# Eight clamps of a weight-narrowing chain issued from GpSimd instead of VectorE

## The chip, the cores and the metric

The kernel runs on one core of a Trainium2 chip. The metric is the device time of one execution in microseconds (us); before the change it is 867.72 us, the median of three runs (867.5 to 868.18).

## The reference

The inputs are `q`, `k`, `v` of shape (4, 8, 576, 64), and two pairs of weights `w_in` (512 x 2048) and `w_out` (2048 x 512). What is computed is a retention attention followed by two dense layers:

```python
scores = scale * np.matmul(q, k.transpose(0, 1, 3, 2))
ret = scores * Dmat[None]            # gamma_h ** (i - j) below the diagonal
x = np.matmul(ret, v)                # to (2304, 512) tokens
h = x @ w1_in;  x = np.maximum(0.01 * h, h) @ w1_out
h = x @ w2_in;  out = (h - np.tanh(h)) @ w2_out
```

The weights arrive as 64-bit floats, seen on the chip as 64-bit words; everything else is 32-bit.

## The kernel before, in words

The work has two parts. `retention()` goes over 16 pairs of heads (four batches of four pairs), and from pair 5 on it interleaves layer 1's first weight group with them, in twelve "units". `layers()` then does the rest of the two layers, and is bound to the order that a list of steps gives. Every engine executes its instructions in the order in which the program issues them; the order is written out by hand (`tc.manual_schedule()`).

**Pairs.** In pair i the program issues: the loads of pair i + 2 on SyncE's queue; `scores(i)` (TensorE, line 632, into the single PSUM tile `sc`); `prep_q(i)` (GpSimd, lines 602 and 607, two products that scale q in place); `mask(i)` (VectorE, line 646, two products from `sc`, which must be done before `scores(i + 1)` may write `sc`); then fillers; then `pair_steps(i)`, which has a unit's first matmuls `unit_h(u)` (line 758, into the single PSUM tile `x_b`), fillers, the second matmuls of the unit before, `unit_o(u - 1)` (line 783), then the outputs of pair i - 1 (lines 697 and 708), the states of pair i (lines 665, 673, 675), the copies out of PSUM (lines 716, 717), the mask of the tail (line 655) and the preparation of pair i + 1 (lines 621, 613); then fillers again. Behind `unit_h(u)` ScalarE and VectorE read `x_b` (lines 764 to 766), so `unit_h(u + 1)` must wait for line 766 of unit u.

**Fillers.** `fill(i, part)` issues the next stretch of a list of operations that narrows weight pieces from 64 to 32 bits. The first 8 pieces of the list are layer 1's first weight group: pieces 0 and 1 are the first two input blocks, 2 and 3 the first two output blocks, 4 and 5 input, 6 and 7 output. `narrow_ops` gives five operations for each piece:

- `begin` (ScalarE, line 166): the absolute value of the top words goes to a tile `cw`. The pool of `cw` has two buffers here, so `begin` of piece n + 2 waits until the split of piece n has read its tile.
- `clamp` (VectorE, line 172): `cw` is bounded from below and above, in place.
- `shift` (VectorE, line 177): a shift and a bit mask, in place.
- `top` and `low` (VectorE, line 183, twice): the sign and the low bits are joined in from the landed 64-bit words.

`split_piece` follows later: ScalarE rounds `cw` into a matmul weight (line 255), GpSimd subtracts for the low part (line 256). Between a piece's `shift` and its `top` stands the split of the piece before. Which operation falls into which pair is set by the list `at_pair = [0, 4, 9, 15, 22, 34, 46, 52]`. For what follows, by that list: `clamp` 0 is issued in pair 1; `low` 0, `clamp` 1 and `shift` 1 in pair 2; split 0, `top` 1, `low` 1 and `clamp` 2 in pair 3; `shift` 2, split 1, `top` 2, `low` 2 and `clamp` 3 in pair 4; `shift` 3, split 2, `top` 3, `low` 3 and then, behind `unit_h(0)`, `clamp` 4 and the rest of piece 4 in pair 5; pieces 5 and 6 in pair 6, piece 7 in pair 7, and split 7 in pair 8.

**Who needs them.** `unit_h(0)` in pair 5 and `unit_h(1)` in pair 6 multiply by pieces 0 and 1, `unit_o(0)` in pair 6 by pieces 2 and 3, `unit_h(2)` in pair 7 by pieces 4 and 5, and `unit_o(2)` in pair 8 by pieces 6 and 7. Later pieces are narrowed by the same `narrow_ops`, 56 of them with a clamp, and keep VectorE for it.

Of the kernel before, what the change touches and what calls it, by code (L numbers as in the profile page):

```python
# [35 lines left out]
def retention_moe_moe(  # L36
# [16 lines left out]
    nc = tc.nc  # L53
# [9 lines left out]
    GF = 4  # L63
# [88 lines left out]
    def narrow_ops(key):  # L152

        if not wide:
            def only():
                w = cw_pool[0].tile([P, 512], F32, tag="cw", name="cw")
                nc.vector.tensor_copy(out=w, in_=raw.pop(key))
                half[key] = w
            return [only]
        t = {}  # L160

        def begin():
            words = raw.pop(key).bitcast(U32).rearrange("p (n t) -> p n t", t=2)
            t["lo"], t["hi"] = words[:, :, 0], words[:, :, 1]
            t["w"] = cw_pool[0].tile([P, 512], U32, tag="cw", name="cw")
            nc.scalar.activation(  # L166
                out=t["w"].bitcast(F32), in_=t["hi"].bitcast(F32), func=AF.Abs
            )

        def clamp():  # L170
            wf = t["w"].bitcast(F32)
            nc.vector.tensor_scalar(  # L172
                out=wf, in0=wf, scalar1=F64_LO, scalar2=F64_HI, op0=ALU.max, op1=ALU.min
            )

        def shift():
            nc.vector.tensor_scalar(
                out=t["w"], in0=t["w"], scalar1=3, scalar2=0x3FFFFFF8,
                op0=ALU.logical_shift_left, op1=ALU.bitwise_and,
            )  # L180

        def join(src, scalar, op):
            nc.vector.scalar_tensor_tensor(  # L183
                out=t["w"], in0=t[src], scalar=scalar, in1=t["w"], op0=op, op1=ALU.bitwise_or
            )

        def top():
            join("hi", 0xC0000000, ALU.bitwise_and)

        def low():  # L190
            join("lo", 29, ALU.logical_shift_right)
            half[key] = t["w"].bitcast(F32)

        return [begin, clamp, shift, top, low]

    def keep_split(key, wf):
# [916 lines left out]
```

## Time and profile before

| | |
|---|---|
| median of three runs | 867.72 us (867.5 to 868.18) |
| the profiled execution, whole | 868.1 us |
| its span, first to last instruction | 866.1 us |
| mean granted TensorE clock | 0.998 of full speed |
| busy: TensorE | 850.1 us (98%) |
| busy: VectorE | 604.1 us (70%) |
| busy: ScalarE | 451.2 us (52%) |
| busy: GpSimd | 377.1 us (44%) |

The profile is one execution. Its time of 868.1 us is 0.38 us above the median, and 2.0 us of it lie outside the span. Times within the span count from its first instruction. In a timeline row the columns are start, duration, engine, line, operation, output from inputs, shapes and the number of merged instructions; the bracket at the end says how long the engine sat idle ahead of the row, and what released it. Engine names there are PE (TensorE), PEld (its weight loads), DVE (VectorE), ACT (ScalarE), POOL (GpSimd) and SP (SyncE).

### The profile page before, as it was taken

The numbers are of one execution on the slowest core, as the hardware profiler recorded it, in microseconds if no ns is written. First come the engines' busy times: TensorE is split into PE (matmuls) and PEld (weight loads), VectorE is DVE, ScalarE is ACT, GpSimd is POOL, SyncE is SP. The second block draws the span as 40 slices with busy tenths as digits, with TensorE's granted clock in tenths as the row PEclk, the third lists the DMA queues.
The fourth block names the chain that finished last, engine by engine and source line by source line (L and its number), as shares of the span: only waits on it lengthen the run. The fifth ranks groups of instructions, "written<-read, shape, count | busy, mean of one in ns | idle before, by whom it ended". The sixth has DMA issues, their size and how long they took to land.

```text
span 866.1 us, 15237 instructions
## 1 busy us (share of the span) xinstructions
PE 850.1 (98%) x5728; PEld 748.2 (86%) x5728; DVE 604.1 (70%) x1038; ACT 451.2 (52%) x899; POOL 377.1 (44%) x304
## 2 busy tenths in 40 slices
PE   6999999999999999999999999999999999999997
PEld 5889999888888889888888898888999899999996
DVE  5995767587786676658765577756676667777675
ACT  4553444453255433454444577666556566566663
POOL 2541222040036302464365379655545445545553
PEclk9999999999999999999999999999999999999999
DMA  9835663433454533644444503572225412563112
GB/s 340 315 125 172 219 209 118 150 121 103 135 213 186 179 121 110 243 170 127 190 175 165 195 1 146 226 284 75 75 96 180 162 73 74 208 231 121 49 50 74
DMA packets 38778, 134.43 MB, mean 155 GB/s; under 512 B 4400, under 2 KB 5936, under 8 KB 36656
## 3 DMA queue, kind: packets, MB, share of 16 engines
q1 hardware_dynamic: 38272, 133.25, 43.7%
q8 instruction: 45, 0.74, 0.4%
q14 instruction: 29, 0.24, 0.1%
q10 hardware_dynamic: 432, 0.20, 0.1%
HBM read 97.26 MB, written 36.18 MB: 154 GB/s over the span
## 4 chain that ended last, share of the span: by engine, by line
PE 89%; DVE 4%; DMA 2%; issue 2%; POOL 1%; ACT 1%; POOLq 0%; ACTq 0%; SPq 0%; DVEq 0%
PE a L428 40%; PE h L275 22%; PE h L309 17%; PE a L783 3%; PE x_b L758 3%; PE o L708 1%; PE sc L632 1%; PE o L697 1%; DVE cw L183 1%; DMA acc<-in_w1i 1%; DMA cm_sb<-in_cmask 1%; DVE pt L646 1%; PE x_c L665 0%; DVE v L394 0%; DMA kt_sb<-in_ktab 0%
## 5 line engine op out<-in xcount | busy, mean ns | idle before, releaser
L428 PE MATMUL a<-w 128*128 128x512 f32 (+1 forms) x1680 | 395.2, 377 | 0.5 <-POOL w L400 0.5
L428 PEld LDWEIGHTS a<-w 128*128 128x128 f32 x1680 | 293.1, 188 | 48.9 <-POOL w L400 1.3
L256 POOL TENSOR_TENSOR w<-cw,w 128x512 fp32r<-128x512 f32 x80 | 113.5, 1436 | 233.6 <-ACT w L255 207.8
L275 PE MATMUL h<-xh,w 128*128 128x512 f32 (+1 forms) x672 | 187.1, 349 | 0.0
L368 POOL TENSOR_TENSOR v<-t,u 128x512 f32<-128x512 f32 (+1 forms) x76 | 93.1, 1225 | 100.5 <-ACT t L365 96.4
L275 PEld LDWEIGHTS h<-xh,w 128*128 128x128 f32 x672 | 119.5, 188 | 17.0
L400 POOL TENSOR_TENSOR w<-v,w 128x512 fp32r<-128x512 f32 (+1 forms) x76 | 96.1, 1265 | 63.9 <-ACT w L399 63.9
L354 ACT ACTIVATE w<-h 128x512 fp32r<-128x512 f32 (+1 forms) x68 | 37.2, 547 | 160.3 <-PE h L275 115.4
L275 PE MATMUL h<-xl,w 128*128 128x512 f32 (+1 forms) x336 | 117.0, 348 | 0.0
L309 PE MATMUL h<-xh,w 128*128 128x256 f32 x512 | 100.9, 281 | 0.2
L309 PEld LDWEIGHTS h<-xe,w 128*128 128x128 f32 x576 | 80.8, 189 | 10.7 <-DVE mk L303 3.1
L183 DVE SCALAR_TENSOR_TENSOR cw<-st,cw 128x512 uint32<-128x512 uint32 x96 | 86.4, 900 | 2.5
L394 DVE SCALAR_TENSOR_TENSOR v<-q,v 128x512 f32<-128x512 f32 (+1 forms) x76 | 60.8, 800 | 37.1 <-POOL v L368 37.1
L364 ACT ACTIVATE u<-h 128x512 f32<-128x512 f32 (+1 forms) x80 | 44.2, 553 | 80.4 <-DVE h L303 53.2
L309 PEld LDWEIGHTS h<-xh,w 128*128 128x128 f32 x512 | 83.1, 190 | 2.8 <-DVE v L397 1.5
L309 PE MATMUL h<-xe,w 128*128 128x256 f32 x576 | 84.3, 282 | 1.1 <-DVE mk L303 1.0
L505 DVE TENSOR_TENSOR acc<-a,acc 128x512 f32<-128x512 f32 (+1 forms) x114 | 72.1, 657 | 18.5 <-PE a L428 18.5
L399 ACT ACTIVATE w<-v 128x512 fp32r<-128x512 f32 (+1 forms) x76 | 45.3, 596 | 61.5 <-DVE v L397 59.0
L172 DVE TENSOR_SCALAR cw<-cw 128x512 f32<-128x512 f32 x64 | 33.1, 518 | 57.7 <-ACT cw L166 57.6
L309 PE MATMUL h<-xl,w 128*128 128x256 f32 x256 | 71.8, 281 | 0.0
L275 PEld LDWEIGHTS h<-xl,w 128*128 128x128 f32 x336 | 63.3, 188 | 8.6
L383 DVE TENSOR_TENSOR h<-h,t 128x512 f32<-128x512 f32 (+1 forms) x80 | 51.3, 641 | 15.2 <-ACT t L365 15.2
(82 smaller groups left out, 1159.8 us busy)
## 6 DMA issues: line engine op xcount, KB each, us to landing
kept<-w SPq DMA_DIRECT2D x48, 512.0 KB, 3.5
w<-kept SPq DMA_DIRECT2D x48, 512.0 KB, 4.8
xe<-xkept SPq DMA_DIRECT2D x12, 1536.0 KB, 6.7
st<-in_w2i SPq DMA_DIRECT2D x16, 512.0 KB, 3.5
st<-in_w1i SPq DMA_DIRECT2D x12, 512.0 KB, 4.1
st<-in_w1o SPq DMA_DIRECT2D x12, 512.0 KB, 3.5
xkept<-xe SPq DMA_DIRECT2D x4, 1536.0 KB, 6.7
kv<-in_vn SPq DMA_DIRECT2D x16, 320.0 KB, 5.2
```

Source lines behind the costliest of these rows:

```text
L183: nc.vector.scalar_tensor_tensor(out=t["w"], in0=t[src], scalar=scalar, in1=t["w"], op0=op, op1=ALU.bitwise_or)
L256: nc.gpsimd.tensor_tensor(out=wp[:, 1, :], in0=wf, in1=wp[:, 0, :].bitcast(F32), op=ALU.subtract)
L275: nc.tensor.matmul(out=ps[:, :n], lhsT=w[:, wi, cs], rhs=x[:, kk, t0:t0 + n], start=kk == 0 and i == 0, stop=kk == KK - 1 and i == 2,)
L309: nc.tensor.matmul(out=out_, lhsT=w[:, wi_, at:at + P], rhs=x(xi, kk), start=start and kk == 0 and j == 0, stop=stop and kk == 1 and j == ...
L364: nc.scalar.activation(out=u[:, :n], in_=h, func=AF.Square)
L368: nc.gpsimd.tensor_tensor(out=v[:, :n], in0=t_[:, :n], in1=u[:, :n], op=ALU.mult)
L383: nc.vector.tensor_tensor(out=h, in0=h, in1=tmp[s][1][:, :n], op=ALU.subtract)
L394: nc.vector.scalar_tensor_tensor(out=v, in0=q, scalar=RHO_A, in1=v, op0=ALU.add, op1=ALU.mult)
L399: nc.scalar.activation(out=gt[:, 0, g_at(s)], in_=v, func=AF.Copy)
L400: (nc.gpsimd if m else nc.vector).tensor_tensor(out=gt[:, 1, g_at(s)], in0=v, in1=gt[:, 0, g_at(s)].bitcast(F32), op=ALU.subtract)
L428: nc.tensor.matmul(out=o, lhsT=l, rhs=r, start=f == 0 and i == 0 and d % pack == 0, stop=f == GF - 1 and i == 2 and (d + 1) % pack == 0, s ...
L505: nc.vector.tensor_tensor(out=dst, in0=a, in1=dst, op=ALU.add)
```

## The change

The clamp of the eight pieces (layer 0 in the code, blocks 0 to 3 of both kinds; `GF` is 4) is issued from GpSimd; all other operations, their order in the program and the other 56 clamps stay.

```diff
         def clamp():
             wf = t["w"].bitcast(F32)
-            nc.vector.tensor_scalar(
+            (nc.gpsimd if key[0] == 0 and key[2] < GF else nc.vector).tensor_scalar(
                 out=wf, in0=wf, scalar1=F64_LO, scalar2=F64_HI, op0=ALU.max, op1=ALU.min
             )
```

## Rows read from the trace of the kernel before

**Rows 1.** The page, busy time, share and instructions by engine.

```profile
PE 850.1 (98%) x5728; PEld 748.2 (86%) x5728; DVE 604.1 (70%) x1038; ACT 451.2 (52%) x899; POOL 377.1 (44%) x304
```

**Rows 2.** Stretches: bounds, length, busy time by engine, granted clock, DMA share, GB/s.

```profile
18.00:30.00 12.00, 9.34 (x147) 7.58 (x142) 11.66 (x25) 7.92 (x23) 8.21 (x8) 1.00 1.04 374
...
66.00:866.00 800.00, 793.54 (x5023) 698.48 (x5021) 550.94 (x919) 416.76 (x815) 349.00 (x274) 1.00 0.42 147
```

**Rows 3.** Timeline of PE, 28 to 65 us.

```profile
28.53 0.49 PE L638 MATMUL x_e<-bd,qk 128*128 128x128 f32 x2
30.12 1.16 PE L632 MATMUL sc<-qk 64*128 64x128 f32 x16 [1.10 <-DVE pt L646]
...
38.47 0.39 PE L758 MATMUL x_b<-xh,w 128*128 128x256 f32 x1
...
51.46 0.50 PE L758 MATMUL x_b<-xh,w 128*128 128x256 f32 x2 [0.86 <-POOL w L256]
...
64.86 1.45 PE L783 MATMUL a<-w 128*128 128x256 f32 x10 [0.28 <-POOL w L256]
```

**Rows 4.** Timeline of DVE, 18 to 38 us.

```profile
18.01 1.29 DVE L646 TENSOR_TENSOR pt<-sc,cm_sb 128x512 f32<-128x512 f32 x2 [0.68 <-DMA cm_sb<-in_cmask]
...
21.95 0.43 DVE L172 TENSOR_SCALAR cw<-cw 128x512 f32<-128x512 f32 x1
...
24.09 0.94 DVE L183 SCALAR_TENSOR_TENSOR cw<-acc,cw 128x512 uint32<-128x512 uint32 x1
...
26.92 1.31 DVE L183 SCALAR_TENSOR_TENSOR cw<-acc,cw 128x512 uint32<-128x512 uint32 x1
...
28.73 1.29 DVE L646 TENSOR_TENSOR pt<-sc,cm_sb 128x512 f32<-128x512 f32 x2
...
32.45 1.53 DVE L183 SCALAR_TENSOR_TENSOR cw<-acc,cw 128x512 uint32<-128x512 uint32 x2
...
35.56 0.73 DVE L177 TENSOR_SCALAR cw<-cw 128x512 uint32<-128x512 uint32 x1
36.33 1.42 DVE L183 SCALAR_TENSOR_TENSOR cw<-acc,cw 128x512 uint32<-128x512 uint32 x2
37.66 0.68 DVE L766 TENSOR_TENSOR w<-x_b,w 128x512 fp32r<-128x512 f32 x1
```

**Rows 5.** Groups of DVE by shape, 11 to 66 us: the eight clamps.

```profile
L172 DVE TENSOR_SCALAR cw<-cw 128x512 f32<-128x512 f32 x8 | 4.8, 600 | 0.1
```

**Rows 6.** Timeline of POOL, 13 to 36 us.

```profile
13.87 0.32 POOL L607 TENSOR_TENSOR qk<-qk,qt_sb 128x64 f32<-128x64 f32 x1
...
26.41 1.27 POOL L602 TENSOR_TENSOR qk<-qk,qt_sb 128x512 f32<-128x512 f32 x1
27.64 0.77 POOL L607 TENSOR_TENSOR qk<-qk,qt_sb 128x64 f32<-128x64 f32 x1
28.97 1.28 POOL L256 TENSOR_TENSOR w<-cw,w 128x512 fp32r<-128x512 f32 x1 [0.56 <-ACT w L255]
31.41 1.29 POOL L602 TENSOR_TENSOR qk<-qk,qt_sb 128x512 f32<-128x512 f32 x1 [1.16 <-PE sc L632]
...
34.73 1.28 POOL L256 TENSOR_TENSOR w<-cw,w 128x512 fp32r<-128x512 f32 x1 [1.29 <-ACT w L255]
```

**Rows 7.** Groups of POOL by shape, whole span: busy, mean ns, idle before.

```profile
L368 POOL TENSOR_TENSOR v<-t,u 128x256 f32<-128x256 f32 x12 | 8.9, 738 | 1.8 <-PE a L428 1.2 <-ACT t L365 0.6
```

**Rows 8.** Timeline of ACT, 21 to 32 us.

```profile
21.11 0.66 ACT L166 ACTIVATE cw<-acc 128x512 f32<-128x512 f32 x1
...
26.48 0.70 ACT L166 ACTIVATE cw<-acc 128x512 f32<-128x512 f32 x1 [0.26 <-POOL w L256]
...
31.00 0.65 ACT L166 ACTIVATE cw<-acc 128x512 f32<-128x512 f32 x1
```

**Rows 9.** Timeline of SP: the issue of pair 5's k.

```profile
23.42 0.44 SPq L588 DMA_DIRECT2D qk<-in_kT  x1
```

**Rows 10.** DMA issues, 23.3 to 23.6 us: KB, median us to landing.

```profile
qk<-in_kT SPq DMA_DIRECT2D x1, 288.0 KB, 5.3
```

## The prediction

> **What bounds the kernel now.** I read the page first: TensorE is busy 850.1 of the 866.1 us of the span [rows 1], so all that an edit outside TensorE can give is in the gaps of that engine. The stretches say where these are: behind 66 us TensorE is busy 793.54 of 800 us, and the eight clamps lie ahead of that; from 18 to 30 us it is busy 9.34 of 12, while VectorE is busy 11.66 and the DMA engines are full (a share of 1.04) [rows 2]. So the edit falls into the one stretch where VectorE is the busiest compute engine. What matters is whether TensorE reaches the dense part earlier.
>
> TensorE's timeline answers that. At 30.12 us it starts `scores(5)` after 1.10 us of idling, released by `mask(4)` on VectorE. From there it runs without a gap until 51.46 us, where it sat idle 0.86 us for the split of piece 5, and it waits 0.28 us at 64.86 us for the split of piece 7 [rows 3]. The weak points of the change are therefore `mask(4)`, then `unit_h(1)` at 38.47 us, then the two splits. `unit_h(1)` shows no gap, but only just: line 766, which has to read `x_b` first, runs from 37.66 to 38.34 us [rows 4], 0.13 us ahead of it.
>
> VectorE's timeline shows the chain behind `mask(4)`. `mask(2)` at 18.01 us waits 0.68 us for a transfer, and after that the engine has no idle time in these rows through line 766 [rows 4]. The third thing to see is that VectorE and GpSimd hold each other up: the join at 26.92 us takes 1.31 us, where the pair at 36.33 us takes 1.42 for two [rows 4], and GpSimd's long product ran from 26.41 to 27.68 us; its 64-column product behind that took 0.77 us, against 0.32 for the same shape at 13.87 us [rows 6]. Joins, which read two SBUF tiles, and GpSimd's instructions do not run side by side here; I replay them as taking turns.
>
> **The change, part by part.** Off VectorE come eight clamps of 0.60 us in the mean, 4.8 us together [rows 5]. Onto GpSimd come eight clamps that no row shows. Bounds for one: GpSimd's product of two tiles takes 0.32 us at 64 columns and 1.27 at 512 [rows 6], and 0.738 at 256 [rows 7]. That is a line of some 0.21 us plus 2.07 ns a column. A clamp reads one tile of 512 columns, so it lies between 0.32 and 1.27 us; with half the slope, as for one operand instead of two, it is an estimate of 0.21 + 512 x 1.04 ns = 0.74 us. I take 0.75 and keep both ends.
>
> The Trainium skill (GPSIMD Engine Reference, Engine selection) says to do elementwise max on VectorE, as GpSimd is about half as fast with two inputs, though near line rate with one; by its 1.03 cycles an element at 1.2 GHz (Elementwise side-by-side) the columns take 0.44 us, an estimate of 0.65 us with 0.21 of start, and the sum below would be about +0.3 instead of +0.6 us. No row here has a one-input instruction of that size on GpSimd.
>
> Each clamp also becomes a hand-over ScalarE to GpSimd to VectorE, for which I take 0.06 us a step; `mask(4)`'s end at 30.02 us [rows 4] and the start of `scores(5)` at 30.12 [rows 3] are 0.10 apart. On GpSimd it stands in front of the next `prep_q` and split. Nothing is added to SyncE's queue, and no transfer is issued elsewhere. Now the clamps one by one.
>
> Clamp 0 is worth nothing: its 0.43 us turn into more idle time ahead of `mask(2)`, which a transfer releases at 18.01 us [rows 4].
>
> Clamp 1: `begin` 1 ends at 21.77 us [rows 8], as before. GpSimd is idle then, clamps from 21.83 to 22.58, and `shift` 1 starts at 22.64 instead of some 22.4 us: `mask(3)` is 0.23 us later. The loss is absorbed one instruction on: `top` 1 at 24.09 us takes 0.94 us, not 0.7 [rows 4], since it waits for GpSimd's product anyway, so it ends at about 25.03 us as now.
>
> Clamp 2 is where something is won. Its `begin` starts at 26.48 us and ends at 27.18 [rows 8], so GpSimd, held by a clamp that waits, no longer starts `prep_q(4)` at 26.41 us [rows 6]. The join at 26.92 us then has no competitor: 0.69 instead of 1.31 us [rows 4]. Clamp 2 itself is off VectorE too. `mask(4)` follows the join at 27.63 and ends at 28.92 instead of 30.02 us. The transfer of k for `scores(5)` was issued at 23.42 us [rows 9] and takes 5.3 us [rows 10], so it is there at 28.7; TensorE's preceding matmuls end at 29.02 us [rows 3]. `scores(5)` starts at about 29.05 instead of 30.12 us: 1.07 us won, and no more than the 1.10 us of idling can be.
>
> Then the price. GpSimd gets to `prep_q(4)` at 28.25 instead of 26.41 us and, with `shift` 2 in between, to split 1 at some 30.2 instead of 28.97 us [rows 6]; it ends at 31.5 us, when `unit_h(0)`, moved up by 1.07 us, needs that weight at about 31.8. `begin` 3 reuses the tile that split 1 frees, so it runs from 31.55 to 32.2 us instead of starting at 31.00 [rows 8]. Clamp 3 then falls between the joins of piece 2, which ran at 32.45 us [rows 4]: the first join from 31.9, the clamp from 32.5 to 33.25, the second join to 33.9, against 33.98 us now. So the lead of VectorE is down to 0.4 us at `shift` 3 (35.8 instead of 36.29 us [rows 4] at its end).
>
> Behind clamp 3 `prep_q(5)` goes from 33.85 us instead of 31.41, and split 2, which ran at 34.73 [rows 6], starts at 35.75 us, right behind `shift` 3. It holds up `top` 3, which ran at 36.33 us after that split was over [rows 4]: now the joins go from 37.0 to 38.3, and line 766 ends at 39.0 instead of 38.34 us. `unit_h(1)` starts at 39.1 instead of 38.47 us: the 1.07 us are given back and 0.6 us more.
>
> Clamps 4 to 7 come when TensorE is the slower engine. The replay goes on 0.6 us later everywhere. Split 5 keeps its 0.86 us of idling, since it comes at the end of ScalarE's in-order work behind the matmuls of the same pair, and split 7's 0.28 us stays by the like. The sum is +0.6 us on the profiled 868.1 us. Rounded down a little for the turns that may fall the other way, I add 0.5 to the median of 867.72 us, which is 0.38 below the profiled execution: **868.2 us**. About 0.2%, or 1.7 us, is what a measurement of this kernel can tell from no change.
>
> **The rivals.**
>
> Rival A, the gain is kept. `top` 3 gets its turn ahead of split 2, or the clamp is short: line 766 ends a microsecond earlier, and nothing behind gives it back. For it: the 1.31 us join [rows 4] and the wait of 1.10 us [rows 3] are plain. Against it: line 766 has 0.13 us to spare today, so all of the lead has to survive 9 us of taking turns. Its time is 867.72 - 1.1 = 866.6 us, and 0.28 us less if split 7 came earlier as well.
>
> Rival B, GpSimd becomes the bound. With a clamp of 1.27 us or more, clamp 1 ends at 23.1 us, `mask(3)` is 0.76 us late, and `top` 1 comes just after GpSimd has gone from `prep_q(3)` to split 0: it waits to 26.0 and ends at 26.65 instead of 25.03 us. Clamp 2 ends at 28.1, `prep_q(4)` behind it blocks the next join, and `mask(4)` ends at 31.4 instead of 30.02 us; the same again at clamp 3 makes `unit_h(1)` 1.9 us late: 869.6 us. The point from which it decides is about 1.1 us a clamp. Two passes over the tile, 2 x 1.27 = 2.5 us, would cost some 5 us: 872.7 us. For it: every long GpSimd instruction that the rows show is at 1.27 us or more [rows 6], and the clamp has two operations. Against it: they all read two tiles. The skill's rule above, VectorE for elementwise work, would be borne out in this case.
>
> Rival C, nothing reaches TensorE, or the clamps aren't where the diff puts them: 867.7 us.
>
> **How the numbers follow.** The forecast, gain and return with -0.3 to +1.2 us net, has 0.52; A 0.18; B 0.22, of which two thirds are beyond 1.7 us; C 0.08. Faster by over 0.2% would take more than the 1.10 us that can be won at `scores(5)` and 0.28 besides: 0.04. Slower by over 0.2% is most of B with a little of the forecast: 0.16. The rest, 0.80, is no difference. The range goes from A, 866.6, to B at a clamp of 1.27 us with some more, 870.0 us; what it leaves out is the slow clamp and a gain above A.
>
> **What would show it.** Right: line 172 on GpSimd eight times at 0.6 to 0.9 us, 56 times on VectorE; the join near 27 us at 0.7 us; `scores(5)` near 29.1 us; a TensorE wait of about a microsecond ahead of `unit_h(1)`, released by line 766, where none is now. Wrong: a clamp over 1.1 us, a `top` 1 that ends past 26 us, or `scores(5)` later than 30.1 us (B); `unit_h(1)` near 37.5 us and a span a microsecond shorter (A).

## The result and the profile after

The changed kernel took 874.35 us in the median (872.53 to 875.4, four runs) against 867.93 us (867.5 to 868.18) for the kernel before: a ratio of 1.0072, 95% interval 1.0054 to 1.009. It is slower by 6.4 us; 868.2 us and a range up to 870.0 had been forecast. The profiled execution took 874.7 us, with a span of 872.6 us, 6.5 us more than before. All comparisons below are ratios to runs of the kernel before made beside them, as single executions of that kernel spread from 867.5 to 870.4 us over the series.

The page of the changed kernel, busy time by engine, answers to [rows 1]:

```profile
PE 853.2 (98%) x5728; PEld 750.9 (86%) x5728; DVE 603.6 (69%) x1030; ACT 451.1 (52%) x899; POOL 393.9 (45%) x312
```

TensorE does the same 5728 matmuls in 853.2 instead of 850.1 us, 3.1 us more, and idles 872.6 - 853.2 = 19.4 instead of 16.0 us, 3.4 us more. So the 6.5 us more of span have two halves: longer waits, and slower matmuls. GpSimd has gained 16.8 us of work with eight instructions; VectorE has lost eight and is busy only 0.5 us less.

The instructions of line 172 in the changed kernel (count, shortest, median and longest in ns, first and last start) answer to [rows 5]:

```profile
L172 DVE TENSOR_SCALAR cw<-cw x56: 410/420/1516, 84.3 to 439.7; 128x512 f32<-128x512 f32 x56
L172 POOL TENSOR_SCALAR cw<-cw x8: 1914/2123/2452, 14.1 to 58.5; 128x512 f32<-128x512 f32 x8
```

A clamp on GpSimd takes 1.91 us at the least and 2.12 in the median. Its estimate was 0.74 us, and its upper bound 1.27. Where this ends up is seen on the timeline of PE in the changed kernel, beside [rows 3]:

```profile
26.61 2.08 PE L632 MATMUL sc<-qk 64*128 64x128 f32 x16 [2.56 <-DVE pt L646]
28.61 1.52 PE L697 MATMUL o<-qk,st 64*64 64x128 f32 x12
...
32.50 1.16 PE L632 MATMUL sc<-qk 64*128 64x128 f32 x16
...
42.23 0.39 PE L758 MATMUL x_b<-xh,w 128*128 128x256 f32 x1 [1.31 <-DVE w L766]
...
55.07 0.39 PE L758 MATMUL x_b<-xh,w 128*128 128x256 f32 x1 [1.21 <-ACT w L255]
...
56.43 0.50 PE L758 MATMUL x_b<-xh,w 128*128 128x256 f32 x2 [0.86 <-POOL w L256]
...
62.16 0.87 PE L697 MATMUL o<-qk,st 64*64 64x128 f32 x12
```

Two rows of the kernel before that [rows 3] doesn't show, `scores(4)` and the outputs behind `unit_h(2)`:

```profile
24.61 1.16 PE L632 MATMUL sc<-qk 64*128 64x128 f32 x16 [0.49 <-DMA qk<-in_kT]
...
55.66 0.87 PE L697 MATMUL o<-qk,st 64*64 64x128 f32 x12
```

There are three new waits: 2.56 us ahead of `scores(4)`, which began at 24.61 us in the kernel before after 0.49 us of idling, 1.31 us ahead of `unit_h(1)`, and 1.21 us within `unit_h(2)` ahead of the old 0.86. The 1.10 us ahead of `scores(5)` are gone. Compared at the same matmuls, the delay is 2.0 us at `scores(4)` (26.61 against 24.61), 2.4 at `scores(5)`, 3.8 at `unit_h(1)`, 5.0 at the last of these waits (56.43 against 51.46) and 6.5 us at the outputs behind it (62.16 against 55.66). The last step, 1.5 us, has no wait in it. There the granted clock is low, as it is behind 26.6 us. Stretches of the changed kernel (columns as in [rows 2]):

```profile
27.00:30.00 3.00, 3.00 (x28) 2.53 (x26) 2.85 (x9) 0.55 (x2) 2.59 (x2) 0.50 0.90 342
57.00:60.00 3.00, 3.00 (x18) 3.00 (x17) 2.93 (x4) 1.72 (x4) 3.00 (x3) 0.55 0.00 0
```

The column ahead of the last two is the clock: 0.50 of full speed is 1.2 GHz. `scores(4)` takes 2.08 us there, and 1.16 in the kernel before. Both stretches come just behind the idling of 2.56 us and of 1.21 and 0.86 us. Some 1.6 us are lost in the first and 1.5 us in the second: that is the 3.1 us of slower matmuls.

VectorE's timeline in the changed kernel shows where the first wait comes from, beside [rows 4]:

```profile
17.91 1.29 DVE L646 TENSOR_TENSOR pt<-sc,cm_sb 128x512 f32<-128x512 f32 x2 [0.70 <-DMA cm_sb<-in_cmask]
...
23.71 1.48 DVE L177 TENSOR_SCALAR cw<-cw 128x512 uint32<-128x512 uint32 x1 [1.90 <-POOL cw L172]
25.22 1.29 DVE L646 TENSOR_TENSOR pt<-sc,cm_sb 128x512 f32<-128x512 f32 x2
...
29.04 0.69 DVE L183 SCALAR_TENSOR_TENSOR cw<-acc,cw 128x512 uint32<-128x512 uint32 x1
...
37.69 1.48 DVE L177 TENSOR_SCALAR cw<-cw 128x512 uint32<-128x512 uint32 x1 [0.49 <-POOL cw L172]
39.20 2.37 DVE L183 SCALAR_TENSOR_TENSOR cw<-acc,cw 128x512 uint32<-128x512 uint32 x2
41.50 0.68 DVE L766 TENSOR_TENSOR w<-x_b,w 128x512 fp32r<-128x512 f32 x1
```

Two things add up ahead of `mask(3)` at 25.22 us: `shift` 1 waits 1.90 us for the clamp, and then takes 1.48 us instead of the 0.43 of the kernel before:

```profile
22.41 0.43 DVE L177 TENSOR_SCALAR cw<-cw 128x512 uint32<-128x512 uint32 x1
```

The second is seen on GpSimd, which goes straight from the clamp to `prep_q(3)` (timeline of POOL in the changed kernel):

```profile
21.76 1.92 POOL L172 TENSOR_SCALAR cw<-cw 128x512 f32<-128x512 f32 x1 [1.63 <-ACT cw L166]
23.64 1.26 POOL L602 TENSOR_TENSOR qk<-qk,qt_sb 128x512 f32<-128x512 f32 x1
...
47.64 2.35 POOL L172 TENSOR_SCALAR cw<-cw 128x512 f32<-128x512 f32 x1
49.96 1.29 POOL L256 TENSOR_TENSOR w<-cw,w 128x512 fp32r<-128x512 f32 x1
```

`shift` 1 starts just after the product, and ends 0.29 us after it (25.19 and 24.90 us): the product holds it up. So the clamp makes VectorE arrive just after GpSimd's next instruction has started, and VectorE pays for that one too. The same happens to `shift` 3 at 37.69 us (0.49 us of waiting, 1.48 us long), ahead of the joins and of line 766 that `unit_h(1)` waits for.

The wait of 1.21 us within `unit_h(2)` runs through ScalarE (timeline of ACT in the changed kernel):

```profile
51.29 0.69 ACT L166 ACTIVATE cw<-acc 128x512 f32<-128x512 f32 x1 [1.44 <-POOL w L256]
...
54.40 0.62 ACT L255 ACTIVATE w<-cw 128x512 fp32r<-128x512 f32 x1
```

Split 4, the row at 49.96 us above, comes right behind clamp 5. `begin` 6 waits for its tile until 51.29 us (45.75 us in the kernel before), and ScalarE's part of split 5, behind it in that engine's order, starts at 54.40 instead of 49.43 us.

### The profile page after: what moved, and what is told of

The parts are those of the page before. It is cut to its first block, busy times and chain, and to the rows that moved or that the text cites. A ratio compares the mean times of both kernels' runs of the same rounds, so it can differ in the third digit from the quotient of the medians.

```text
span 872.6 us, 15234 instructions
## 1 busy us (share of the span) xinstructions
PE 853.2 (98%) x5728; PEld 750.9 (86%) x5728; DVE 603.6 (69%) x1030; ACT 451.1 (52%) x899; POOL 393.9 (45%) x312
## 4 chain that ended last, share of the span: by engine, by line
PE 90%; POOL 2%; DMA 2%; DVE 2%; issue 1%; ACT 1%; SPq 0%; POOLq 0%; ACTq 0%; DVEq 0%
PE a L428 39%; PE h L275 21%; PE h L309 17%; PE a L783 3%; PE x_b L758 3%; PE sc L632 2%; PE o L708 1%; PE o L697 1%; POOL cw L172 1%; DMA qk<-in_kT 1%; DMA qk<-in_qT 1%; POOL w L256 1%; PE x_c L665 1%; DMA kt_sb<-in_ktab 0%; DMA kv<-in_vn 0%
## 5 line engine op out<-in xcount | busy, mean ns | idle before, releaser
L172 DVE TENSOR_SCALAR cw<-cw 128x512 f32<-128x512 f32 x56 | 29.4, 526 | 57.7 <-ACT cw L166 57.4
```

## The experiments

There are twelve kernels besides the changed one, with four to eleven executions each. Their ratios to the kernel before are, with 95% intervals:

| kernel | ratio | interval |
|---|---|---|
| changed kernel | 1.0072 | 1.0054 to 1.009 |
| one bound only on GpSimd | 1.003 | 1.002 to 1.004 |
| eight clamps left out | 0.9994 | 0.9984 to 1.0003 |
| clamp of a spare tile beside | 1.0009 | 0.9996 to 1.0021 |
| gap filled with matmuls | 1.0043 | 1.0028 to 1.0058 |
| only pieces 0 to 3 on GpSimd | 1.0035 | 1.0023 to 1.0047 |
| only pieces 4 to 7 on GpSimd | 1.0002 | 0.9992 to 1.0012 |
| all but piece 1 on GpSimd | 1.0044 | 1.0027 to 1.006 |
| three `cw` tiles | 1.0036 | 1.0024 to 1.0048 |
| 160 columns only | 0.9988 | 0.9979 to 0.9998 |
| all but piece 1, three tiles | 1.000 | 0.999 to 1.0009 |
| clamps twice on VectorE | 1.0015 | 1.0005 to 1.0025 |
| clamp split by columns | 0.9987 | 0.9978 to 0.9996 |

**What a clamp on GpSimd costs.** One bound, and 160 columns (both edits against the kernel before; `(...)` marks arguments cut here):

```diff
+            if key[0] == 0 and key[2] < GF:
+                nc.gpsimd.tensor_scalar(
+                    out=wf, in0=wf, scalar1=F64_LO, scalar2=None, op0=ALU.max
+                )
+                return
             nc.vector.tensor_scalar(...)
```

> The changed kernel with GpSimd taking only the lower bound (max); the upper bound (min) of these eight pieces is left out. Theory 'two operations': the 1.91 us of the clamp are two operations after one another, so with one it takes about 1.0 us, mask(3) ends about 0.9 us earlier than in the changed kernel and the kernel lands near 868.5 to 869.5 us. Rival 'form': the price is that of the instruction form over 512 columns, the clamp stays at 1.9 us and the kernel near 874 us.

```diff
+            if key[0] == 0 and key[2] < GF:
+                nc.gpsimd.tensor_scalar(
+                    out=wf[:, :160], in0=wf[:, :160], scalar1=F64_LO, scalar2=F64_HI,
+                    op0=ALU.max, op1=ALU.min
+                )
+                return
             nc.vector.tensor_scalar(...)
```

> The changed kernel with GpSimd clamping 160 of the 512 columns of the eight tiles (the other columns are left unclamped): the hand-over and the order are kept, the price comes near the 0.75 us that the prediction took. Theory 'only the price was wrong': the clamp takes 0.6 to 0.9 us and the kernel lands where the prediction's replay put it, 0 to 1.2 us above the kernel before. Rival 'the replay was wrong too': the extra hand-over and the turns cost more than that, 2 us or more above the kernel before.

The clamps in the kernel with one bound, and then in the kernel with 160 columns (columns as for line 172 above):

```profile
L173 POOL TENSOR_SCALAR cw<-cw x8: 1479/1522/2011, 14.6 to 56.9; 128x512 f32<-128x512 f32 x8
```

```profile
L173 POOL TENSOR_SCALAR cw<-cw x8: 740/972/1283, 14.5 to 52.8; 128x160 f32<-128x160 f32 x8
```

By the shortest of each, 352 columns more cost 1.914 - 0.740 = 1.17 us, 3.3 ns a column, which leaves 0.21 us of start. That start is what GpSimd's products gave; the slope is not. The second bound costs 1.914 - 1.479 = 0.435 us, 0.85 ns a column. So neither expectation for one bound was right: an operation has its price, but with a single one the 512 columns still take 1.48 us, more than the product of two tiles. The kernel with one bound came to 1.003, about 2.6 us, a little less than half of the loss.

The kernel with 160 columns is the test of the replay, since its clamp costs, at the shortest, the 0.74 us that the prediction had taken (0.97 us in the median). It came out 0.12% faster than the kernel before, about a microsecond; the replay had said 0.6 us slower. Its timelines, DVE first:

```profile
26.80 0.69 DVE L189 SCALAR_TENSOR_TENSOR cw<-acc,cw 128x512 uint32<-128x512 uint32 x1
27.52 1.29 DVE L652 TENSOR_TENSOR pt<-sc,cm_sb 128x512 f32<-128x512 f32 x2
...
31.53 1.42 DVE L189 SCALAR_TENSOR_TENSOR cw<-acc,cw 128x512 uint32<-128x512 uint32 x2
...
34.68 2.37 DVE L189 SCALAR_TENSOR_TENSOR cw<-acc,cw 128x512 uint32<-128x512 uint32 x2
36.97 0.68 DVE L772 TENSOR_TENSOR w<-x_b,w 128x512 fp32r<-128x512 f32 x1
```

Then GpSimd's clamp of piece 3, and PE:

```profile
31.83 0.99 POOL L173 TENSOR_SCALAR cw<-cw 128x160 f32<-128x160 f32 x1 [0.78 <-DMA qk<-in_kT]
```

```profile
28.91 1.16 PE L638 MATMUL sc<-qk 64*128 64x128 f32 x16
...
37.71 0.39 PE L764 MATMUL x_b<-xh,w 128*128 128x256 f32 x1 [0.24 <-DVE w L772]
```

The join ahead of `mask(4)` takes 0.69 us and `scores(5)` starts at 28.91, as the replay had it (0.69 and 29.05). The two joins of piece 2 take 1.42 us together, from 31.53 to 32.95 us, and the clamp of piece 3 runs beside them, from 31.83 to 32.82 us and 0.25 us longer than its shortest. The replay had put it between them, as a turn of its own; the joins did not wait for it. `top` 3 and `low` 3 are held up by split 2, as assumed (2.37 us), but all of it happens a microsecond earlier, and `unit_h(1)` starts at 37.71 instead of 38.47 us.

**What VectorE's clamps cost before.** They are left out, and in another kernel done twice:

```diff
         def clamp():
             wf = t["w"].bitcast(F32)
+            if key[0] == 0 and key[2] < GF:
+                return
```

> The kernel before with the eight clamps left out altogether: what they cost on VectorE, and with that the most that a free clamp elsewhere could bring. Theory of the prediction: mask(4) ends about a microsecond earlier, scores(5) starts near 29.1 us, and 1.0 to 1.4 us come off (866.4 to 866.9 us). Rival: the wait moves to a transfer or to unit_h(1), and it stays within 0.5 us of the kernel before.

```diff
             nc.vector.tensor_scalar(...)
+            if key[0] == 0 and key[2] < GF:
+                nc.vector.tensor_scalar(
+                    out=wf, in0=wf, scalar1=F64_LO, scalar2=F64_HI, op0=ALU.max, op1=ALU.min
+                )
```

> The kernel before with each of the eight clamps issued twice on VectorE: 4.8 us more work on the engine that is busiest from 18 to 60 us. Theory 'VectorE has slack where its clamps stand' (after leaving them out brought nothing): within 1 us of the kernel before. Rival 'VectorE is the bound of the stretch': scores(5) and unit_h(1) come later by the clamps ahead of them, 1.5 to 2.5 us.

Leaving them out brought nothing that can be measured. DVE in that kernel:

```profile
23.27 1.29 DVE L648 TENSOR_TENSOR pt<-sc,cm_sb 128x512 f32<-128x512 f32 x2 [0.82 <-DMA cm_sb<-in_cmask]
...
27.32 1.32 DVE L185 SCALAR_TENSOR_TENSOR cw<-acc,cw 128x512 uint32<-128x512 uint32 x1
28.67 1.29 DVE L648 TENSOR_TENSOR pt<-sc,cm_sb 128x512 f32<-128x512 f32 x2
```

In this execution `mask(3)` waits for a transfer instead, and the join ahead of `mask(4)` still meets GpSimd's product and takes 1.32 us, so `mask(4)` starts at 28.67 us where it started at 28.73. So the relief of VectorE alone wins nothing here. What the kernel with 160 columns has besides is GpSimd held ahead of `prep_q(4)`, and with that the short join. Twice the clamps cost 0.15%, about 1.3 us, between the two expectations. Its profiled execution, at 871.71 us, lies near the top of its runs (868.3 to 872.0) and isn't read here.

**Waiting for the clamp, or GpSimd's time.** VectorE keeps its clamp, and GpSimd clamps a spare stretch of `acc` at the same place (set to 1.0 once at the start):

```diff
             nc.vector.tensor_scalar(...)
+            if key[0] == 0 and key[2] < GF:
+                spare = acc_t[:, 0, NT - 512:]
+                nc.gpsimd.tensor_scalar(
+                    out=spare, in0=spare, scalar1=F64_LO, scalar2=F64_HI, op0=ALU.max, op1=ALU.min
+                )
```

> The kernel before, clamps on VectorE, and GpSimd clamps a tile of its own at each of the eight places, which nobody waits for. Theory 'hand-over': the loss comes from VectorE waiting for the clamp, so this costs at most 2 us (under 870 us). Rival 'occupancy': the loss comes from what stands behind the clamp on GpSimd (prep_q, the splits) and from turns with VectorE, so most of the 6.4 us come back here (872 us or more).

The ratio is 1.0009, at most 1.0021, with clamps of 1.91 us on GpSimd. Set against the loss of 0.72%, the time that GpSimd spends is thus at most some 30% of it; the rest needs somebody who waits for the clamp. The ten executions lie apart, though, four at 867.6 to 868.6 and six at 870.3 to 871.2 us, so that the clamps beside are free is not shown. The test isn't quite clean, since the spare clamp doesn't wait for `begin` either and so starts earlier in some pairs.

**Which pieces.** The edits from here to the clock are against the changed kernel.

```diff
-            (nc.gpsimd if key[0] == 0 and key[2] < GF else nc.vector).tensor_scalar(
+            (nc.gpsimd if key[0] == 0 and key[2] < 2 else nc.vector).tensor_scalar(
```

> Only pieces 0 to 3 are clamped on GpSimd, 4 to 7 on VectorE again. Theory: the two stalls up to unit_h(1) stay (3.8 us at 38.5 us of the kernel before), those at unit_h(2) go, so 871.5 to 872 us. Rival: the later half carries the loss since TensorE's earlier idle is made up for, under 870 us.

```diff
-            (nc.gpsimd if key[0] == 0 and key[2] < GF else nc.vector).tensor_scalar(
+            (nc.gpsimd if key[0] == 0 and 2 <= key[2] < GF else nc.vector).tensor_scalar(
```

> Only pieces 4 to 7 are clamped on GpSimd. Theory: split 5 arrives late for unit_h(2) as in the changed kernel, 1.2 us of idling and up to 1.5 us at the lower clock behind it, so 869 to 870.5 us. Rival: without the delay of the first half there is slack, and it stays within 0.5 us of the kernel before.

The first four cost 0.35%, the last four nothing that can be measured (1.0002), and all eight 0.72%: the halves don't add up. Alone, the last four make a wait of 0.47 us within `unit_h(2)` in that kernel's profile, against 1.21 us in the changed kernel. The reading is that they cost when the first four have made the same chain late; no run tests it by itself.

```diff
-            (nc.gpsimd if key[0] == 0 and key[2] < GF else nc.vector).tensor_scalar(
+            (nc.gpsimd if key[0] == 0 and key[2] < GF and key != (0, 0, 1) else nc.vector).tensor_scalar(
```

> The changed kernel, but piece 1 is clamped on VectorE again. Theory: the 2.56 us ahead of scores(4) and the lower clock behind them come from clamp 1 alone, so scores(4) starts near 24.6 us and 2 us or more come off (872.4 us or less). Rival: the next clamps make the same wait one pair later, and less than 1 us comes off.

```diff
-            cw_pool[0] = ac.enter_context(tc.tile_pool(name="c0", bufs=2))
+            cw_pool[0] = ac.enter_context(tc.tile_pool(name="c0", bufs=3))
```

> The changed kernel with three cw tiles instead of two, so that begin of a piece no longer waits for the split of the piece two ahead. Theory: the loss at unit_h(2) runs through that wait (begin 6 stands ahead of split 5 on ScalarE and waits for split 4), so the 1.21 us there go and 1 to 2.5 us come off (872 to 873.4 us). Rival: the clamps' own 1.9 us on GpSimd set it, and it stays at 874.4 us.

Taken by itself, leaving clamp 1 on VectorE takes away some 2.4 us of the loss and the third tile some 3.1 us, each to within 2 us or so, and each at the place that was expected. PE without clamp 1 on GpSimd, and then with three tiles:

```profile
24.55 1.16 PE L632 MATMUL sc<-qk 64*128 64x128 f32 x16 [0.49 <-DMA qk<-in_kT]
```

```profile
54.34 0.51 PE L758 MATMUL x_b<-xh,w 128*128 128x256 f32 x2 [0.86 <-POOL w L256]
```

`scores(4)` has its old wait of 0.49 us back, and with three tiles the wait of 1.21 us within `unit_h(2)` is gone while that of 0.86 stays. The third tile gave more than the 1 to 2.5 us expected: in its profile the wait ahead of `unit_h(1)` is down to 0.57 us as well, and the clock is full all through, behind 2.55 us of idling too. That execution is one of the two fastest of its seven (870.62 to 873.16 us). Both edits together:

> The changed kernel with piece 1 clamped on VectorE and three cw tiles: two of the three places of the loss are taken out. Theory 'three places': the wait ahead of scores(4) and the 1.21 us at unit_h(2) are both gone, what stays is the wait ahead of unit_h(1) of about 1.2 us, so 1 to 2 us above the kernel before. Rival: taking one wait away only moves it to the next, and 3 us or more stay, as with either alone.

They give 1.000 (0.999 to 1.0009): seven clamps on GpSimd, each at its full price, cost nothing. PE in that kernel:

```profile
24.90 1.16 PE L632 MATMUL sc<-qk 64*128 64x128 f32 x16 [0.50 <-DMA qk<-in_kT]
...
29.73 1.16 PE L632 MATMUL sc<-qk 64*128 64x128 f32 x16 [0.42 <-DVE pt L646]
...
38.65 0.39 PE L758 MATMUL x_b<-xh,w 128*128 128x256 f32 x1 [0.27 <-DVE w L766]
...
51.65 0.51 PE L758 MATMUL x_b<-xh,w 128*128 128x256 f32 x2 [0.87 <-POOL w L256]
```

and its clamps, with `begin` 6 and split 5 on ACT:

```profile
L172 POOL TENSOR_SCALAR cw<-cw x7: 1915/2100/2358, 13.8 to 53.3; 128x512 f32<-128x512 f32 x7
```

```profile
45.47 0.68 ACT L166 ACTIVATE cw<-acc 128x512 f32<-128x512 f32 x1
...
49.62 0.61 ACT L255 ACTIVATE w<-cw 128x512 fp32r<-128x512 f32 x1
```

So the expectation of 1 to 2 us was too high: the wait ahead of `unit_h(1)` went with the other two, down to 0.27 us. `begin` 6 starts at 45.47 us without a wait. By these runs the idling is made of two couplings: `shift` 1, on the engine that `mask(3)` stands on, waits for clamp 1; and `begin` of a piece, in ScalarE's order, waits for the split of the piece two ahead, which the clamps on GpSimd make late. The low clock comes on top, and with the idling gone it is gone too: this execution has the full clock throughout. The third tile in the kernel before was not run, so what it gives by itself is not shown.

**The clock.** In the changed kernel, the tail's scores of pair 3 are multiplied six times, in the gap ahead of `scores(4)`:

```diff
             def scores_tail(i):
-                nc.tensor.matmul(
-                    out=x_a, lhsT=qk[i][:, 0, S - CH:], rhs=bds[i % 2], start=True, stop=True
-                )
+                for _ in range(6 if i == 3 else 1):
+                    nc.tensor.matmul(
+                        out=x_a, lhsT=qk[i][:, 0, S - CH:], rhs=bds[i % 2], start=True, stop=True
+                    )
```

> The changed kernel with the tail scores of pair 3 multiplied six times instead of once (the same result each time), about 2.3 us of matmuls in the 2.56 us that TensorE idles ahead of scores(4). Theory 'clock': the matmuls from 26.6 to 30.1 us run at the higher level again (scores(4) 1.16 us instead of 2.08), and 1 to 1.5 us come off (872.9 to 873.4 us). Rival: the clock is not what costs there, since unit_h(1) waits for VectorE anyway, and the kernel stays at 874.4 us.

Work added to TensorE made the kernel faster: 1.0043 against 1.0072, about 2.5 us, to within 2 us or so. The repeats took 1.60 us in all, and PE in that kernel ran at full speed behind them:

```profile
24.78 1.60 PE L639 MATMUL x_e<-bd,qk 128*128 128x128 f32 x12
27.41 1.16 PE L632 MATMUL sc<-qk 64*128 64x128 f32 x16 [1.02 <-issue]
28.50 0.87 PE L698 MATMUL o<-qk,st 64*64 64x128 f32 x12
```

More came off than the 1 to 1.5 us expected: in that profile the clock is also full from 57 to 63 us, behind waits of 1.21 and 0.87 us that are as long as in the changed kernel. The edit doesn't touch that place, so whether the filling did this or the execution had it so is open. The clock on record for each execution, as a mean over it, says that the changed kernel had less of it every time: 0.994 to 0.996 in its four executions, and 0.997 to 1.0 in the four of this one. But the clock doesn't follow every gap: in the kernel with the first four pieces on GpSimd, the wait ahead of `scores(4)` is 2.62 us, and the stretch behind it is at full speed:

```profile
27.00:30.00 3.00, 3.00 (x50) 2.47 (x50) 2.85 (x9) 0.55 (x2) 2.45 (x2) 1.00 0.93 353
```

That execution took 869.71 us; the other nine of the same kernel took 870.43 to 874.09 us.

**The clamp split between the engines.** GpSimd clamps 160 columns and VectorE the other 352, so nothing is left out (against the kernel before, whose call it replaces):

```diff
+            parts = [(nc.vector, wf)]
+            if key[0] == 0 and key[2] < GF:
+                parts = [(nc.gpsimd, wf[:, :160]), (nc.vector, wf[:, 160:])]
+            for engine, part in parts:
+                engine.tensor_scalar(
+                    out=part, in0=part, scalar1=F64_LO, scalar2=F64_HI, op0=ALU.max, op1=ALU.min
+                )
```

> The whole computation, with each of the eight clamps split: GpSimd takes columns 0 to 159, VectorE columns 160 to 511 beside it. If the 0.1% that the short clamp brought comes from GpSimd being held in front of prep_q(4), so that the join ahead of mask(4) runs alone, some of it stays: 0.3 to 0.9 us below the kernel before. Rival: VectorE's 352 columns cost about 0.35 us each on the same path and take it back, and it stays within 0.3 us of the kernel before.

It is 0.13% faster than the kernel before, with an interval of 0.04 to 0.22%: a gain of about a microsecond, at the limit of what can be told. The fastest executions are closer, 867.33 us here and 867.69 us for the kernel before beside it. Its profiled execution took 870.9 us, above its ten other runs (867.33 to 868.6), so the mechanism can't be read from it and isn't shown.

## Why the prediction was wrong

**The step that failed is the price of the clamp.** The prediction took the line of the products, 0.21 us plus 2.07 ns a column, and halved the slope because a clamp reads one tile instead of two. The start was right. The slope is 3.3 ns a column with two bounds and 2.5 with one (1.479 less the same 0.21 us, over 512 columns), more than three times and more than twice the 1.04 estimated. The upper bound of 1.27 us, the whole product, didn't hold it either: operations were not counted in it, and a product's one operation was taken to be dearer than a clamp's two because of its operand. With 1.91 us the clamp lies halfway between that bound and the rival's two passes at 2.5 us.

The Trainium skill (GPSIMD Engine Reference, Engine selection) was right in the rule, elementwise work on VectorE (the move cost 0.72%), but here not in the price that it attaches, one-input operations at roughly line rate. The estimate from its 1.03 cycles an element at 1.2 GHz (Elementwise — side-by-side cycle accounting) is 0.86 ns a column; 3.3 ns were measured.

**Rival B is what happened**, with its chance of 0.22, and as it was drawn: the clamp over 1.1 us, `mask(3)` late, `unit_h(1)` late. It had `mask(3)` 0.76 us late and the delay growing at `top` 1; the run shows 2.0 us of delay already at `scores(4)`, since `shift` 1 is held up by the clamp and by the product behind it. By the two points that it gave, 1.9 us at 1.27 us a clamp and 5 us at 2.5, it would have given some 3.5 us at 1.91 us. The idle time did grow by 3.4 us. That the two agree is in part luck, as the waits fell in other places than it had them: `top` 1 took 0.72 us and the join ahead of `mask(4)` 0.69 us in the changed kernel, neither held up. What it lacked were the 3.1 us of the lower clock.

**The clock was not among the steps.** The page of before had it at full speed nearly everywhere (0.998 in the mean), and the cost of a gap beyond its length was put at nothing. In the profiled execution it was 3.1 of the 6.5 us.

**The replay beyond the price** was half right. The kernel with 160 columns shows the gain at `mask(4)` as predicted, and its mechanism, the join without a competitor. It shows the return of that gain at `unit_h(1)` as wrong: there the two joins of piece 2 ran without a turn for the clamp, which ran beside them. At the price that was assumed, rival A (866.6 us, a gain of 1.1 us) was the outcome, in a kernel that leaves 352 columns of the eight tiles unclamped.

**What was right:** clamp 0 costs nothing (`mask(2)` starts at 17.91 us in the changed kernel, released by its transfer as before); the 0.86 us ahead of split 5 stay in every kernel; and no kernel here won more than about 1.1 us. That VectorE's load holds the stretch, which was read from its 11.66 of 12 us [rows 2], is borne out one way only: leaving eight clamps out gave 0.9994, adding as many 1.0015.

## What to carry to other kernels

An instruction moved to another engine has to be priced from a row of that instruction on that engine; operands and columns of its neighbours there bound it badly. When a move to an idle engine puts a hand-over into a chain, count the wait of the receiver, then what the new engine starts next, and then who waits for the buffers that are freed later: here a third tile and one piece left where it was made the same seven instructions free. And a busy engine need not be the bound: leave the work out once, and see whether anything comes off.

## What was not expected of the hardware

GpSimd's clamp of one tile (1.91 us for 128x512, 1.48 us with one operation) takes longer than its product of two (1.27 us). Waits of TensorE were followed by matmuls at 1.2 GHz in some executions (2.56 us, and 1.21 with 0.86 us, in the changed kernel) and not in others (2.62 us with the first four pieces on GpSimd, 2.55 us with three tiles). Where they were, the slower matmuls cost 3.1 us in one execution, nearly as much as the longer idling (3.4 us). With some 1.1 us more of matmuls in one of the gaps (1.60 us in all) the kernel came out some 2.5 us faster; how much of that is theirs is open.
